# Putting all engines' programs into the entry block without a closing barrier, and issuing the first transfers ahead of the entry barrier

## The chip, the cores and the metric

The kernel runs on one core of one Trainium2 chip. The metric is device time in microseconds (us). The profile's "span" goes from the first to the last instruction of the program; the measured time is longer than it by a rest (1.77 us in the profiled execution of before).

## The reference, cut to what matters

One decode step. A sliding window of attention over a cache (window W = 2048 of 8192 positions, batch 8, 16 key/value heads, 32 query heads, head size 128) and a small MLP (576 to 4608 to 576), mixed by a gate:

```python
q = (x @ wq).reshape(B, 1, 32, 128).transpose(0, 2, 1, 3)
k = repeat(k_cache[:, :, Sk - W:, :], 2, axis=1)      # 67 MB in the window
v = repeat(v_cache[:, :, Sk - W:, :], 2, axis=1)      # 67 MB in the window
p = softmax(einsum("bhqd,bhkd->bhqk", q, k) * Dh ** -0.5)
a = einsum("bhqk,bhkd->bhqd", p, v) ... @ wo
b = gelu(layernorm(x) @ w1 + b1) @ w2 + b2
return g * a + (1 - g) * b                            # g = sigmoid(sum(x * gate_w))
```

With one query per sequence, every byte of the window has to be brought in once. The kernel brings 154.3 MB into the core's memory; its busiest engine, PE, works 69% of the span beside that.

## The kernel before

A planner puts every operation on one engine's list, with its waits; `P.emit` then writes an engine's list out. The parts that the change touches are how the program is opened and how the lists become blocks:

```python
    with ExitStack() as es:
        block = es.enter_context(nc.Block())
        ...
        P.schedule()
        @block.sync
        def _(e):
            P.emit("sp", e, eng_sems, dma_sems)

        @block.gpsimd
        def _(e):
            P.emit("pool", e, eng_sems, dma_sems)
        ... # the same for vector, tensor and scalar
```

What the profile of before shows of this: ahead of the lists, under line 842, four memsets of constants on POOL (96 to 99 ns each), a drain on each of the five engines (7 to 169 ns) and the semaphore instructions of a barrier (17 to 51 ns), the last of them at 0.7 us; behind the lists, under line 223, a branch of the sync engine (42 ns), another drain on each engine (13 to 461 ns) and the semaphore instructions of one more barrier (17 to 51 ns, at 367.4 to 367.5 us). Below, the first group is called the entry block and the entry barrier, the second the end block and the closing barrier.

The first transfers on the lists, and the last operation:

```python
d_x = dma("act", lambda e: e.dma_start(x_sb, x2), "x", ...)
d_gw, d_gw1 = ...            # gate_w, on the Scalar engine's queue
d_b1 = dma("act", ...)
d_wqr = dma("sp", lambda e: e.dma_start(wq_r, A_wq[512:576, :]...), "wq", ...)   # 512 KB
d_wqm = dma("sp", lambda e: e.dma_start(wq_m..., A_wq[0:512, :]...), "wq", ...)  # 4 MB
d_w1m, d_w1r = ...           # 4.5 MB and 576 KB of w1, on the same queue
...                          # then K, V, wo, b2, w2, all on the sync engine's queue
fin.append(dma(eng, ... out2[:, JN * j:JN * j + JN] ...))   # one output DMA each from sync and Scalar engine
add("sp", lambda e: None, deps=fin, name="final_wait", cost=0.05)
```

The last line makes the sync engine wait until both output transfers have landed.

## Time and profile before

| | before |
|---|---|
| measured time, median of 6 runs (lowest to highest) | 369.18 us (369.00 to 369.29) |
| profiled execution: measured time, span | 369.27 us, 367.5 us |
| bytes moved, rate over the span | 154.59 MB, 421 GB/s |
| time that the sync engine's packets took, as a share of the 16 DMA engines' span | 98.6% |
| first packet of wq | 1.82 us after the start of the span |
| last packets of the output | 366.68 us |

These are lines of the page of the kernel before. The second gives busy time, share of the span and number of instructions for each engine; the fourth gives, for the sync engine's queue, packets, megabytes and the share of the 16 DMA engines' time; the fifth splits the chain of work that ended last by what it waited for.

```profile
span 367.5 us, 4111 instructions
PE 254.8 (69%) x1815; PEld 87.3 (24%) x1429; DVE 210.1 (57%) x253; ACT 47.8 (13%) x117; POOL 37.6 (10%) x163
...
DMA packets 11851, 154.59 MB, mean 421 GB/s; under 512 B 1292, under 2 KB 1332, under 8 KB 3000
...
q1 hardware_dynamic: 11776, 154.29, 98.6%
...
DMA 74%; DVE 12%; PE 11%; SPq 1%; ACT 1%; issue 1%; DVEq 0%; ACTq 0%
```

The engines have time to spare (PE, the busiest, works 69%) and the queue has almost none (98.6%). From 20 to 350 us the stream brought in 429 GB/s, at a DMA share of 1.01; that a higher rate could not be had is not shown by any run. At this rate the time is: what passes before the first byte, plus 154.3 MB at the stream's rate, plus what passes after the last byte.

The two ends, then. This is the timeline of the kernel before at its start (start us, duration us, engine, line, operation; SPq and ACTq are the sequencers of the sync and the Scalar engine, and a DMA line there is the issue, not the transfer):

```profile
0.31 0.10 POOL L842 MEMSET const-float32-0.0<- 128x1 f32 x1 [0.31 <-issue]
...
0.79 0.39 SPq L401 DMA_DIRECT2D arena<-in_A_wq_dram  x1
0.79 0.59 ACTq L395 DMA_DIRECT2D arena<-in_A_x_dram  x1
1.24 0.42 SPq L402 DMA_DIRECT2D arena<-in_A_wq_dram  x1
...
1.70 0.42 SPq L404 DMA_DIRECT2D arena<-in_B_w_dram  x1
...
9.24 0.29 DVE L411 COPY arena<-arena 8x64 bf16<-8x64 bf16 x2 [9.24 <-DMA arena<-in_gate_w_dram]
```

And these are the instructions of the entry block, asked for by their source line (duration ns as min/median/max, then first and last start in us):

```profile
L842 SPq DRAIN  x1: 7/7/7, 0.0 to 0.0; - x1
...
L842 ACTq DRAIN  x1: 8/8/8, 0.1 to 0.1; - x1
...
L842 POOLq DRAIN  x1: 169/169/169, 0.4 to 0.4; - x1
...
L842 SPq EVENT_SEMAPHORE  x1: 17/17/17, 0.7 to 0.7; - x1
```

The reader should see a sync engine that is ready at 0.0 us, needs 7 ns for its drain, and then waits in the barrier, where POOL with its constants is the last to end its drain (at 0.54 us; the other four end theirs by 0.32). It is let go at 0.7 us, when nothing that it is about to issue needs those constants.

The end, in the same two views; line 223 is the line that opened the block, so its instructions are those of the closing branch and of the end block:

```profile
364.18 0.96 PE L559 MATMUL ps<-arena 128*8 128x288 bf16 x10 [0.66 <-DMA arena<-in_B_w_dram]
...
365.28 0.45 DVE L783 CAST arena<-ps 8x288 bf16<-8x288 f32 x1 [9.86 <-PE ps L559]
365.69 0.31 ACTq L786 DMA_DIRECT2D out_dram<-arena  x1
365.75 0.32 SPq L786 DMA_DIRECT2D out_dram<-arena  x1
```

```profile
L223 ACTq DRAIN  x1: 241/241/241, 366.0 to 366.0; - x1
L223 SPq COMPARE_BRANCH  x1: 42/42/42, 367.1 to 367.1; - x1
L223 SPq DRAIN  x1: 13/13/13, 367.3 to 367.3; - x1
L223 SPq EVENT_SEMAPHORE  x1: 17/17/17, 367.5 to 367.5; - x1
...
L223 PEldq EVENT_SEMAPHORE  x1: 51/51/51, 367.5 to 367.5; - x1
```

The last w2 bytes release PE at 364.18, the outputs are issued at 365.7, and after the first has landed come a branch, a drain and a barrier (from 367.1 to 367.5). The branch is also what waits for the second of the two output transfers (0.2 us in the list of the sync engine's waits).

### The profile page before, as it was taken

The numbers are of one execution on the slowest core, as the hardware profiler recorded it, in microseconds if no ns is written. First come the engines' busy times: TensorE is split into PE (matmuls) and PEld (weight loads), VectorE is DVE, ScalarE is ACT, GpSimd is POOL, SyncE is SP. The second block draws the span as 40 slices with busy tenths as digits, with TensorE's granted clock in tenths as the row PEclk, the third lists the DMA queues.
The fourth block names the chain that finished last, engine by engine and source line by source line (L and its number), as shares of the span: only waits on it lengthen the run. The fifth ranks groups of instructions, "written<-read, shape, count | busy, mean of one in ns | idle before, by whom it ended". The sixth has DMA issues, their size and how long they took to land.

```text
span 367.5 us, 4111 instructions
## 1 busy us (share of the span) xinstructions
PE 254.8 (69%) x1815; PEld 87.3 (24%) x1429; DVE 210.1 (57%) x253; ACT 47.8 (13%) x117; POOL 37.6 (10%) x163
## 2 busy tenths in 40 slices
PE   0349982895598398673986397765966396865995
PEld 0339200131123032010321032111311031214552
DVE  0704699797667754459654764478544864473000
ACT  1010002100300310003000300003100300003200
POOL 7020010011012001000101001010101000000000
PEclk9999998799689879887898879696988789795559
DMA  8999999999999999999999999999999999999994
GB/s 345 428 408 428 428 427 433 432 426 432 435 430 432 422 427 430 432 439 431 426 430 428 422 438 427 430 426 428 433 430 430 428 431 426 433 428 432 418 424 191
DMA packets 11851, 154.59 MB, mean 421 GB/s; under 512 B 1292, under 2 KB 1332, under 8 KB 3000
## 3 DMA queue, kind: packets, MB, share of 16 engines
q1 hardware_dynamic: 11776, 154.29, 98.6%
q8 instruction: 13, 0.21, 0.2%
q10 hardware_dynamic: 56, 0.03, 0.1%
q14 instruction: 6, 0.05, 0.0%
HBM read 154.31 MB, written 0.01 MB: 420 GB/s over the span
## 4 chain that ended last, share of the span: by engine, by line
DMA 74%; DVE 12%; PE 11%; SPq 1%; ACT 1%; issue 1%; DVEq 0%; ACTq 0%
DMA arena<-in_A_k_cache_dram 50%; DMA arena<-in_B_w_dram 15%; DMA arena<-in_A_v_cache_dram 9%; DVE arena L660 9%; PE ps L173 5%; PE ps L516 2%; PE ps L677 1%; DVE arena L605 1%; PE ps L700 1%; SPq L765 1%; ACT arena L619 1%; DVE arena L624 1%; PE ps L518 1%; PE ps L715 1%; DVE arena L614 0%
## 5 line engine op out<-in xcount | busy, mean ns | idle before, releaser
L660 DVE STREAM_TRANSPOSE arena<-arena 128x2048 f32<-128x2048 f32 x64 | 145.2, 2297 | 78.9 <-DMA arena<-in_A_k_cache_dram 71.5
L173 PE MATMUL ps<-arena 128*128 128x512 bf16 x401 | 134.4, 445 | 15.3 <-DVE arena L660 9.8
L677 PE MATMUL ps<-arena 128*128 128x512 bf16 x115 | 51.8, 450 | 16.7 <-DVE arena L660 16.6
L709 ACT ACTIVATE arena<-ps 128x512 f32<-128x512 f32 x32 | 19.1, 598 | 196.7 <-PE ps L700 196.7
L677 PEld LDWEIGHTS ps<-arena 128*128 128x128 bf16 x128 | 14.6, 114 | 125.8 <-issue 66.8
L715 PE MATMUL ps<-arena 128*128 128x8 f32 x256 | 36.9, 275 | 8.7 <-ACT arena L709 7.7
L653 POOL COPY arena<-arena 32x32 bf16<-32x32 bf16 x128 | 26.0, 203 | 159.2 <-PE ps L173 144.6
L715 PEld LDWEIGHTS ps<-arena 128*128 128x128 f32 x256 | 35.6, 217 | 22.4 <-ACT arena L709 16.4
L700 PE MATMUL ps<-arena 128*32 128x512 bf16 x512 | 36.7, 413 | 6.0 <-DMA arena<-in_A_v_cache_dram 6.0
L669 PE MATMUL ps<-arena 128*128 128x512 bf16 x6 | 3.5, 585 | 37.8 <-DVE arena L624 37.8
L605 DVE TENSOR_REDUCE arena<-ps 128x1 f32<-128x2048 f32 x8 | 18.3, 2282 | 15.5 <-PE ps L173 15.5
L619 ACT ACTIVATE arena<-ps,arena 128x512 bf16<-128x512 f32 x32 | 21.6, 686 | 41.4 <-DVE arena L614 41.4
L700 PEld LDWEIGHTS ps<-arena 128*32 128x32 bf16 x512 | 11.3, 100 | 39.8 <-issue 24.1
L624 DVE STREAM_TRANSPOSE arena<-arena 128x512 bf16<-128x512 bf16 x32 | 19.8, 674 | 0.9 <-ACT arena L619 0.9
L733 POOL TENSOR_TENSOR arena<-arena 128x16 bf16<-128x16 f32 x15 | 4.0, 267 | 142.3 <-ACT arena L725 142.3
L516 PE MATMUL ps<-arena 128*128 128x8 bf16 x144 | 10.9, 201 | 4.5 <-DMA arena<-in_B_w_dram 4.5
L559 PE MATMUL ps<-arena 128*8 128x288 bf16 (+1 forms) x140 | 11.6, 315 | 1.9 <-DMA arena<-in_B_w_dram 1.7
L516 PEld LDWEIGHTS ps<-arena 128*128 128x128 bf16 x144 | 10.8, 159 | 5.0 <-DMA arena<-in_B_w_dram 5.0
L669 PEld LDWEIGHTS ps<-arena 128*128 128x128 bf16 x8 | 0.9, 107 | 45.1 <-DVE arena L624 45.1
L733 DVE TENSOR_TENSOR arena<-ps,arena 128x16 bf16<-128x16 f32 x1 | 0.2, 229 | 19.4 <-PE ps L715 19.4
L438 PE MATMUL ps<-arena 8*128 8x8 bf16 x8 | 0.5, 168 | 13.5 <-DVE arena L411 9.8
L631 DVE RECIPROCAL arena<-ps 128x32 f32<-128x32 f32 x8 | 2.9, 358 | 10.5 <-PE ps L629 10.5
(83 smaller groups left out, 95.6 us busy)
## 6 DMA issues: line engine op xcount, KB each, us to landing
arena<-in_A_k_cache_dram SPq DMA_DIRECT2D x32, 2048.0 KB, 35.8
arena<-in_A_v_cache_dram SPq DMA_DIRECT2D x32, 2048.0 KB, 36.7
arena<-in_B_w_dram SPq DMA_DIRECT2D x1, 4608.0 KB, 24.3
arena<-in_A_wq_dram SPq DMA_DIRECT2D x1, 4096.0 KB, 13.1
arena<-in_B_w_dram SPq DMA_DIRECT2D x3, 1296.0 KB, 33.9
arena<-in_B_w_dram SPq DMA_DIRECT2D x2, 576.0 KB, 28.7
arena<-in_A_wq_dram SPq DMA_DIRECT2D x1, 512.0 KB, 3.7
arena<-in_B_w_dram SPq DMA_DIRECT2D x1, 432.0 KB, 30.4
```

The costliest lines, as they stand in the source:

```text
L173: return e.add_instruction(mybir.InstMatmult(name=nc.get_next_instruction_name(), engine=mybir.EngineType.PE, ins=[e.lower_ap(rhs), e.lowe ...
L516: ins = e.matmul(out_, lhsT, yT[:, kt, :], start=(kt == 0), stop=False)
L559: ins = e.matmul(ps[32 * j:32 * j + 8, BK_ACC, 0:JN], lhsT, rhs[:, JN * j:JN * j + JN], start=False, stop=True, skip_group_check=True, til ...
L605: mx = add("dve", lambda e: e.tensor_reduce(out=k(MX), in_=ps[:, 0:4, :].rearrange("p a n -> p (a n)"), axis=AXL.X, op=ALU.max), deps=[qk_ ...
L619: return e.activation(out=Pm[:, 512 * c:512 * c + 512], in_=ps[:, c, :], func=ACTF.Exp, bias=k(NB), scale=SCALE, accum_out=k(SUM + c))
L624: pts.append(add("dve", (lambda c=c: lambda e: e.transpose(bass.AP(arena, offset=aoffs("PT") + 2048 * (g % 2) + 128 * c, ap=[[AST, 128], [ ...
L653: return e.tensor_copy(dst, src)
L660: tr = add("dve", (lambda h=h, kb=kb: lambda e: e.transpose(bass.AP(arena_f, offset=foffs("KT") + kb * 2048, ap=[[AST // 2, 128], [1, 2048]]),
L677: mm = e.matmul(*args, start=False, stop=last) if rc == 0 else held_matmul(nc, e, *args, stop=last)
L700: mm = e.matmul(ps[c:c + 32, BK_OS[i % 2], :], PT[:, g % 2, 512 * q + 32 * t:512 * q + 32 * t + 32], slot(s)[:, 512 * t:512 * t + 512], st ...
L709: u_ev[i] = add("act", lambda e: e.activation(out=EV[:, i % 2, :], in_=ps[:, BK_OS[i % 2], :], func=ACTF.Copy), deps=[prev] + ([u_sum[i - ...
L715: mm = e.matmul(ps[:, BK_S, OC + 16 * (item % 2) + 8 * (q % 2):OC + 16 * (item % 2) + 8 * (q % 2) + 8], EV[:, i % 2, 128 * r:128 * r + 128 ...
```

## The change

Its intent is to take fixed costs off both ends of the stream. There are no blocks any more: all lists are emitted into the entry block, so the branches, the drains of the end block and the closing barrier go (the profile of after has no instruction of line 223). And the first three transfers (two of wq, one of x) are moved in front of their engine's drain, so ahead of the entry barrier. They need nothing that the barrier guards.

```diff
     with ExitStack() as es:
-        block = es.enter_context(nc.Block())
-
         R = {}
 ...
         P.schedule()
-        @block.sync
-        def _(e):
-            P.emit("sp", e, eng_sems, dma_sems)
 ...         (the same for the other four engines)
+        entry = nc.cur_bb.bb.instructions
+        n_entry = len(entry)
+        handles = {"sp": nc.sync, "act": nc.scalar, "pool": nc.gpsimd, "dve": nc.vector, "pe": nc.tensor}
+        for eng in ENGS:
+            P.emit(eng, handles[eng], eng_sems, dma_sems)
+        for etype, count in ((mybir.EngineType.SP, 2), (mybir.EngineType.Activation, 1)):
+            first = [i for i in entry[n_entry:] if i.engine == etype][:count]
+            assert all(isinstance(i, mybir.InstDMACopy) for i in first)
+            for i in first:
+                entry.remove(i)
+            at = next(n for n, i in enumerate(entry) if i.engine == etype and isinstance(i, mybir.InstDrain))
+            entry[at:at] = first
```

The order of work on each engine is otherwise the same.

More of the change, by code (lines that the diff above doesn't have):

```diff
@@ L789, in build_kernel @@
         P.schedule()
-        @block.sync
-        def _(e):
-            P.emit("sp", e, eng_sems, dma_sems)
-        @block.gpsimd
-        def _(e):
-            P.emit("pool", e, eng_sems, dma_sems)
-        @block.vector
-        def _(e):
-            P.emit("dve", e, eng_sems, dma_sems)
-        @block.tensor
-        def _(e):
-            P.emit("pe", e, eng_sems, dma_sems)
-        @block.scalar
-        def _(e):
-            P.emit("act", e, eng_sems, dma_sems)
+        entry = nc.cur_bb.bb.instructions
[10 more added lines that the diff above has]
+            entry[at:at] = first
     return P
```

## The prediction

> **What bounds the kernel now.** The DMA stream. The page gives 154.59 MB at a mean of 421 GB/s over a span of 367.5 us; the sync engine's queue is busy for 98.6% of it. In 10 us windows from 2 to 352 us the DMA share is 0.94 to 1.05 in every one, so the queue never runs dry. [...] PE is busy 69%, DVE 57%; the chain of waits is 74% DMA. Only what lies before the first byte, after the last byte, or changes the rate can change the time.
>
> **The two ends** (timeline, and the entry block's instructions). The sync engine's drain is at 0.0 us, POOL's constant memsets and drain end at about 0.6, the barrier is released at 0.7; the first wq transfer is issued at 0.79 (392 ns on the sequencer), the second at 1.24 (418 ns), w1 at 1.70. The first DMA packets show between 1.7 and 1.8 us, 0.9 us after the first issue. At the end the last w2 data releases PE at 364.18, the output DMAs are issued at 365.69 and 365.75, their wait ends at about 367.1, then come a branch (367.1), a drain (367.3) and the closing barrier (367.4 to 367.5).
>
> **What the change does.**
> 1. Both wq transfers are issued from about 0.0 instead of 0.79 us: about 0.75 us gained at the head of a saturated stream. The barrier moves later: the sync engine spends 0.39 + 0.06 + 0.42 = 0.87 us on its issues before it arrives, so release at 0.9 to 1.05 instead of 0.7, and w1 is issued at about 1.05 instead of 1.70. wq's 4.7 MB are 11 us of stream, so w1 still queues in time.
> 2. POOL's arena memsets start 0.2 to 0.3 us later; x lands earlier, gate_w about as before. Neither matters: the q projection (17.1 us on) and h projection (to 38.6 us) free buffers long before the queue needs them.
> 3. The closing branch, drain and barrier go: 0.35 to 0.4 us after the output wait. [...] The measured 369.21 us is 1.7 us above the span; I assume that this rest stays.
>
> **On the critical path:** nearly all of it, 0.75 at the head (everything later is paced by the stream) and 0.35 at the tail; the 361 us of stream between stay. That is 1.1 to 1.2 us, 0.3%.
>
> **Predicted time:** 368.05 us, 8 in 10 between 367.5 and 368.8. Faster by over 2%: 0.01; within 2%: 0.98; slower by over 2%: 0.01.
>
> **What would show each step.** Head: first wq issue at 0.0 to 0.1 us, first packets at about 0.9. Barrier: released near 1.0. Middle: the same GB/s, the last w2 release 0.7 to 0.8 us earlier (about 363.4). Tail: no drain or barrier after the output wait; span about 366.35 us.
>
> **What would make it wrong.** The measured time may start or end elsewhere than the span, hiding the head start or the missing barrier (then 0.4 or 0.75 us alone). [...] The small loads' new place in the queue, or the thinning out of the stream from 361 to 364 us, may shift by some tenths. A DMA issued as the very first instruction may be slower than 392 ns.

What the forecast's sum came to: the span of 367.5 us, less 1.1 to 1.2 us (0.75 at the head, 0.35 to 0.4 at the tail), is about 366.35 us, and with the rest of 1.7 us on top 368.05 us. The 369.21 us are the median of the three runs of before that were known then. With them went the reason given for the closing barrier being redundant: that it could go was the author's assumption.

## The result, and the profile after

| | before | after |
|---|---|---|
| measured time, median of 6 runs | 369.18 us | 367.71 us |
| lowest to highest | 369.00 to 369.29 | 367.48 to 368.24 |
| profiled execution: measured time | 369.27 us | 367.59 us |
| profiled execution: span | 367.5 us | 366.3 us |
| rest of that execution (measured time minus span) | 1.77 us | 1.29 us |

The ratio of after to before is 0.9962, with a 95% interval of 0.995 to 0.9975; it agrees with the ratio of the means of the six runs (367.77 over 369.16), so it is not quite the ratio of the medians. The change is 0.4% faster: real, and inside the 2% that counts as "same".

The page of the kernel after, the same lines:

```profile
span 366.3 us, 4121 instructions
PE 259.2 (71%) x1837; PEld 87.4 (24%) x1429; DVE 210.1 (57%) x253; ACT 47.8 (13%) x117; POOL 37.5 (10%) x163
...
DMA packets 11851, 154.59 MB, mean 422 GB/s; under 512 B 1292, under 2 KB 1332, under 8 KB 3000
...
q1 hardware_dynamic: 11776, 154.29, 98.9%
...
DMA 74%; DVE 12%; PE 12%; SPq 1%; issue 1%; DVEq 0%
```

Same packets, same bytes, the same limit. (The 22 more PE instructions are not added work: PE's list of operations is the same, so these records are missing from the trace of before.)

Its timeline at the start:

```profile
0.00 0.39 SPq L399 DMA_DIRECT2D arena<-in_A_wq_dram  x1
0.12 0.58 ACTq L393 DMA_DIRECT2D arena<-in_A_x_dram  x1
...
0.45 0.42 SPq L400 DMA_DIRECT2D arena<-in_A_wq_dram  x1
1.27 0.57 ACTq L394 DMA_DIRECT2D arena<-in_gate_w_dram  x2
...
1.27 0.33 SPq L402 DMA_DIRECT2D arena<-in_B_w_dram  x1
...
10.10 0.29 DVE L409 COPY arena<-arena 8x64 bf16<-8x64 bf16 x2 [10.10 <-DMA arena<-in_gate_w_dram]
```

The instructions of the entry barrier, which are now those of line 833:

```profile
L833 POOLq DRAIN  x1: 169/169/169, 0.4 to 0.4; - x1
...
L833 ACTq DRAIN  x1: 138/138/138, 0.7 to 0.7; - x1
L833 SPq DRAIN  x1: 125/125/125, 0.9 to 0.9; - x1
L833 SPq EVENT_SEMAPHORE  x1: 17/17/17, 1.2 to 1.2; - x1
```

And the end, with the waits on semaphores of the sync engine below it (line 153 is the helper that emits all waits; 366.1 is the start of the last one, the wait for both output transfers):

```profile
363.37 0.96 PE L557 MATMUL ps<-arena 128*8 128x288 bf16 x10 [0.61 <-DMA arena<-in_B_w_dram]
...
364.47 0.44 DVE L781 CAST arena<-ps 8x288 bf16<-8x288 f32 x1 [9.70 <-PE ps L557]
364.89 0.31 ACTq L784 DMA_DIRECT2D out_dram<-arena  x1
364.94 0.32 SPq L784 DMA_DIRECT2D out_dram<-arena  x1
```

```profile
L153 SPq EVENT_SEMAPHORE  x39: 17/17/202, 40.7 to 366.1; - x39
```

The first issue moved from 0.79 to 0.00, the last w2 release from 364.18 to 363.37. After the output wait there is nothing left: no branch, no drain, no barrier. The 202 ns are that wait's own record, the last of the program: it starts at 366.14, when the first of the two output transfers has landed, and ends 0.02 us after the second one's last semaphore update, at 366.32.

**Does the head start survive 360 us of stream?** The trace keeps a record of every packet. The sync engine's queue has 11776 packets and 154.29 MB in both traces; sorted by their ends and summed up, they tell when how much had arrived (interpolated between packets; the output's packets are in it, at the very end):

| arrived, MB | before, us | after, us | earlier by, us |
|---|---|---|---|
| first packet starts | 1.82 | 1.02 | 0.80 |
| 0.5 | 3.77 | 3.09 | 0.68 |
| 4.7 (about all of wq) | 13.96 | 13.21 | 0.75 |
| 15 | 37.98 | 37.29 | 0.69 |
| 40 | 96.21 | 95.45 | 0.76 |
| 80 | 189.52 | 188.66 | 0.85 |
| 120 | 282.56 | 281.92 | 0.64 |
| 154.28 | 364.14 | 363.34 | 0.80 |

The lead is 0.64 to 0.85 us at every point of this table, neither eaten up nor grown; packet by packet it wanders between 0.47 and 0.93 us, with a mean of 0.76. That fits a queue that never runs dry (in the trace of before, the DMA share was 0.94 or more in every 10 us window from 2 to 352 us), which leaves no long pause in which a lead could be lost.

**Where the profiled pair's 1.68 us came from.** From the two traces, with the spans to the hundredth (367.54 and 366.35 us; the page rounds them, so the rest comes out 0.04 us smaller here than in the table above):

| piece | before | after | gain |
|---|---|---|---|
| first output transfer landed (start of the sync engine's last wait record) | 366.94 | 366.14 | 0.80 |
| from there to the end of the span | 0.60 | 0.20 | 0.40 |
| rest: measured time minus span | 1.73 | 1.25 | 0.48 |
| sum | 369.27 | 367.59 | 1.68 |

The first row is the head start. The second is the missing branch, drain and barrier: in both kernels its first 0.20 us are the wait for the second output transfer (to 367.14 and 366.35), and only what follows went away, 0.40 us. The third lies outside the span, where the trace has no instruction to show.

**Where the third part lies.** The packed trace also keeps the times at which semaphores were updated (no view prints them; they can be read from the file). The program names semaphores 96 to 122. Semaphore 2 is not among them, yet it is updated nine times in a row just before the program, nine times around or after its end, and nine times once more at the very end. In us from the first instruction:

| | before | after |
|---|---|---|
| nine updates of semaphore 2 ahead of the program | -0.37 to 0.00 | -0.38 to 0.00 |
| last instruction of the program ends | 367.54 | 366.35 |
| next nine updates of semaphore 2 | 367.87 to 368.31 | 364.51 to 366.63, four of them by 365.63 |
| from the program's end to the ninth | 0.77 | 0.29 |
| from the ninth to the last update of all, another nine of semaphore 2 | 1.15 | 1.15 |
| the last update's time, less the measured time | 0.19 | 0.19 |

So the whole 0.48 us lies between the program's end and the ninth update. The nine updates ahead of the program lie at the same distance from its first instruction in both, the time after the ninth is the same, and the last update lies equally far from the measured time, so nothing is left for the start. In the kernel after, four of the nine updates came (364.51 to 365.63 us) before the sync engine was through with the output (its last wait ends at 366.35), so they are taken here not to be the sync engine's; in the kernel before, none came until 0.33 us after the closing barrier.

**The scatter.** The six runs of the changed kernel differ by 0.76 us, those of before by 0.29. Their spans, and what is left of the measured time:

| run of after | 1 | 2 | 3 | 4 | 5 | 6 |
|---|---|---|---|---|---|---|
| measured, us | 367.59 | 368.24 | 367.48 | 367.84 | 367.87 | 367.57 |
| span, us | 366.3 | 367.0 | 366.2 | 366.5 | 366.6 | 366.3 |
| rest, us | 1.29 | 1.24 | 1.28 | 1.34 | 1.27 | 1.27 |

The rest is steady within 0.1 us, so all of the scatter is inside the span. And the profiled run is one of the fast ones: its 1.68 us is a little more than the difference of the medians, 1.47 us.

### The profile page after: what moved, and what is told of

Read it like the earlier page. It is cut to its first block, busy times and chain, and to the rows that moved or that the text cites. A ratio compares the mean times of both kernels' runs of the same rounds, so it can differ in the third digit from the quotient of the medians.

```text
span 366.3 us, 4121 instructions
## 1 busy us (share of the span) xinstructions
PE 259.2 (71%) x1837; PEld 87.4 (24%) x1429; DVE 210.1 (57%) x253; ACT 47.8 (13%) x117; POOL 37.5 (10%) x163
## 3 DMA queue, kind: packets, MB, share of 16 engines
q1 hardware_dynamic: 11776, 154.29, 98.9%
## 4 chain that ended last, share of the span: by engine, by line
DMA 74%; DVE 12%; PE 12%; SPq 1%; issue 1%; DVEq 0%
DMA arena<-in_A_k_cache_dram 50%; DMA arena<-in_B_w_dram 15%; DVE arena L658 9%; DMA arena<-in_A_v_cache_dram 9%; PE ps L173 5%; PE ps L514 2%; PE ps L675 2%; DVE arena L603 1%; PE ps L698 1%; DVE arena L622 1%; SPq L763 1%; PE ps L516 1%; PE ps L713 1%; DVE arena L612 0%; PE ps L667 0%
## 5 line engine op out<-in xcount | busy, mean ns | idle before, releaser
L173 PE MATMUL ps<-arena 128*128 128x512 bf16 x408 | 136.1, 448 | 0.0
L675 PE MATMUL ps<-arena 128*128 128x512 bf16 x128 | 57.4, 449 | 24.3 <-DVE arena L658 24.2
L667 PE MATMUL ps<-arena 128*128 128x512 bf16 x8 | 4.7, 585 | 41.2 <-DVE arena L622 41.2
```

Source lines behind the costliest of these rows:

```text
L173: return e.add_instruction(mybir.InstMatmult(name=nc.get_next_instruction_name(), engine=mybir.EngineType.PE, ins=[e.lower_ap(rhs), e.lowe ...
L675: mm = e.matmul(*args, start=False, stop=last) if rc == 0 else held_matmul(nc, e, *args, stop=last)
```

## The experiments

None of them ran. Five kernels were written and submitted 24 times over more than four hours, under labels from e1 to o1; no chip took any of them. Four are shown here; the fifth was a second control, the changed kernel with the edit below. The expectations say what would tell the explanations apart. None of them is evidence.

What they were to settle is the 0.48 us outside the span. Theory A puts it at the end: without a closing barrier, four engines finish early (in the trace of after their last instructions end at 346.3, 364.3, 364.9 and 365.2 us, the sync engine's at 366.3; in that of before all five end within 0.1 us, in the closing barrier) and are through with whatever follows the program before the sync engine ends. The trace of before shows that something does follow it: nine updates of semaphore 2 within 0.44 us (367.87 to 368.31), and an update of nearly every semaphore from 7 to 255 within 0.66 us (368.21 to 368.87). Theory B puts it at the start, where issuing from the first instruction might hide something that lies before the span. Theory C credits the missing branches and blocks.

One edit was needed in all of them: the four wo loads of the original use a hand-set shape of the destination that could not be built anew, so they were rewritten as a plain access pattern for the same bytes. What that costs no run shows; the 0.5% in the expectations is the author's guess.

```diff
-            src = bass.AP(A_wo.tensor, offset=128 * h0 * D, ap=[[4 * D, 32], [128 * D, WO_CH], [1, 4 * D]])
-            d = dma("sp", lambda e: run_dma(nc, e, dst[:, :, 0:D], src, (AST, ...)),
+            src = bass.AP(A_wo.tensor, offset=128 * h0 * D, ap=[[D, 128], [128 * D, WO_CH], [1, D]])
+            d = dma("sp", lambda e: e.dma_start(dst[:, :, 0:D], src),
```

The control, the kernel before with that edit alone:

> Control. The kernel before, with only the four wo loads written as a plain access pattern (same bytes, same destination, rows of 1152 bytes at the source instead of 4608), because the loads of the original can't be built anew. Both theories: within 0.5% of before, since the stream stays full: 369 to 371 us. All other runs carry the same wo loads and are to be compared with this one. Span 1.7 to 1.8 us below the measured time, as in before.

Not run. Then the open end without the early issue: the changed kernel without its loop that moves instructions.

```diff
-        for etype, count in ((mybir.EngineType.SP, 2), (mybir.EngineType.Activation, 1)):
-            first = ...      (the whole loop of the change)
```

> The entry block without the closing barrier, but nothing issued ahead of the entry barrier. Theory A (the rest of 0.45 to 0.5 us that the change gained outside the span comes from its end: without the closing barrier the other engines are through with whatever follows the program before the sync engine is): span 0.35 to 0.4 us shorter than j1 and measured time minus span 1.25 to 1.35 us, so 0.8 to 0.9 us below j1. Theory B (the rest comes from the start: issuing from the first instruction hides something before the span): only 0.35 to 0.4 us below j1, measured time minus span stays near 1.75 us. First packets at about 1.7 us in both.

Not run. The early issue without the open end: blocks, branches and closing barrier as before, the three transfers moved from their bodies into the entry block.

```diff
+    for eng, etype, count in (("sp", mybir.EngineType.SP, 2), ("act", mybir.EngineType.Activation, 1)):
+        first = [i for i in bodies[eng] if i.engine == etype][:count]
 ...         (a check of what was found; above, each body's list is kept in `bodies`)
+        for i in first:
+            bodies[eng].remove(i)
+        at = next(n for n, i in enumerate(entry) if i.engine == etype and isinstance(i, mybir.InstDrain))
+        entry[at:at] = first
```

> The three transfers issued ahead of the entry barrier, but blocks, branches and closing barrier kept. Theory A: span 0.7 to 0.8 us shorter than j1, measured time minus span near 1.75 us, so 0.7 to 0.8 us below j1. Theory B: the same span, measured time minus span near 1.3 us, so 1.2 to 1.3 us below j1. First packets at about 1.0 us, barrier released at about 1.2 us in both. If the wider scatter of the changed kernel comes from the early issue, it shows here and not in j3.

Not run. The changed kernel with the barrier alone put back, which was meant to split theory A from both others in one run:

```diff
         for eng in ENGS:
             P.emit(eng, handles[eng], eng_sems, dma_sems)
+        nc.all_engine_barrier()
```

> The changed kernel with one barrier of all engines added again at the end of the entry block; no blocks, no branches, the three early transfers stay. The four wo loads are written as a plain access pattern (same bytes and destination), which should cost under 0.5% and not touch either end. Theory A (the 0.45 to 0.5 us that the change gained outside the span come from the missing closing barrier: the other engines are through with whatever follows the program before the sync engine is): measured time minus span goes back to 1.7 to 1.8 us, and the span ends 0.3 to 0.4 us after the output wait. Theory B (they come from the start, where issuing from the first instruction hides something that lies before the span), and theory C (they come from the missing branches and blocks): measured time minus span stays at 1.25 to 1.35 us, the span ends 0.3 to 0.4 us after the output wait as well. Scatter: if the open end makes the wider scatter of the changed kernel (0.76 us over six runs, against 0.29 before), the five runs here scatter by under 0.3 us; if the early issue makes it, by over 0.5 us. In all: first packets at about 1.0 us.

Not run either. So the split of the 1.68 us is read from the two traces. The semaphore updates rule out theory B for the profiled pair: the nine updates ahead of the first instruction are unchanged, and the 0.48 us lie behind the last. They show the overlap of theory A for the nine updates, not for what follows them. How much of the 0.48 us the missing barrier brings and how much the missing branches (theory C) is not separated by any run.

## Why the prediction was right or wrong

The forecast was 368.05 us, between 367.5 and 368.8, within 2%. Measured were 367.71 us. The median lies in the range (one run of the six, 367.48 us, just below it); one term of the sum was wrong, by some 0.4 us, against a forecast gain of 1.1 to 1.2.

1. **The bound: right.** It said that only the two ends or the rate can change the time. The rate is the same (421 and 422 GB/s over the span), and the lead of the stream stays between 0.64 and 0.85 us at all the points of the table.
2. **The head: right, 0.75 us forecast, 0.80 us measured** (issue 0.79 to 0.00, first wq packet 1.82 to 1.02, output wait 366.94 to 366.14). The forecast time of the first packet, 0.9 us, was 0.1 us too early. The packets that it had read at 1.7 to 1.8 us in the trace of before were those of x, on the Scalar engine's queue (1.74); wq's first came at 1.82. The worry that a DMA as the very first instruction might be slow was idle: its issue took 391 ns, against 392 before. From the end of the issue to the first wq packet it was 0.63 us, and 0.65 before; from its start 1.02 and 1.04.
3. **The barrier: right in kind, short in size.** Forecast was a release at 0.9 to 1.05 us and the w1 issue at 1.05; measured were 1.2 and 1.27. The step that failed took the drains as they stood in the entry block before, 7 and 8 ns. Behind a DMA issue the sync engine's drain took 125 ns and started at 0.9, and the Scalar engine's took 138. The trace of before had a hint of this at its other end, where the Scalar engine's drain behind its output DMA took 241 ns. It cost nothing here, as forecast: w1 joined a queue that still held almost all of wq, of which 0.5 MB had arrived by 3.09 us.
4. **"x lands earlier, gate_w about as before": right for x, wrong for gate_w, and harmless.** x was issued 0.67 us earlier (0.12 against 0.79), yet its first packet started at 2.03 us, against 1.74 before, and the first eight packets of 1152 bytes on that queue, which by their order and size are x's eight rows, had arrived by 2.52, against 2.87. gate_w released the Vector engine at 10.10 instead of 9.24. The program waits for x and gate_w together, so moving x gained nothing. From the end of its issue to x's first packet it was 1.34 us, and 0.36 before. In the trace of before, x's packets start 0.08 us ahead of wq's; in that of after, 1.01 us behind them. Why they came so late no run here shows. What it did downstream can be followed: the projection of q began at 17.98 us instead of 17.13, and the sync engine's wait for it grew, as the list of its waits shows (total us, times, longest us), of before and of after:

```profile
SPq L645 <- PE ps L484: 17.0, 1, 17.0
```

```profile
SPq L643 <- PE ps L482: 18.1, 1, 18.1
```

   This wait ends near 22 us. By then 16.3 MB had been put into the queue (wq, w1 and three K loads), and the last of them arrives at about 40 us, an estimate from the table above (15 MB at 37.29, 40 MB at 95.45, so 2.3 us for each further MB). There were some 18 us of slack, and 0.85 us of it were used.
5. **The tail inside the span: right,** 0.35 to 0.4 us forecast, 0.40 measured. The forecast span was 366.35; the profiled one is 366.3, the median of the six is 366.4.
6. **"I assume that this rest stays": wrong.** The measured time was taken as span plus 1.7 us. The rest was 1.77 us in the one execution of before that was profiled, and 1.24 to 1.34 us in all six runs of after. This term, 0.4 to 0.5 us, is why the median lies 0.34 us below the forecast. The prediction named the risk only in one direction: that something outside the span could hide a gain. It did not think of a gain there. What the trace shows in its place: the stretch from the program's end to the ninth update of semaphore 2 shrank from 0.77 to 0.29 us, with four of the nine updates done before the program's end. This is the overlap of theory A, and it leaves no room for theory B; the share of theory C stays open. That the forecast stayed in its range in spite of this owes to the range's width of 1.3 us, not to this step.
7. **The scatter was not forecast.** It lies within the span, over 0.8 us. Which part of the change brings it is open.

## What to carry to other kernels

In this kernel the sync engine's packets took 98.6% of the DMA engines' span and the rate stayed as it was (421 and 422 GB/s over the span); all of the profiled pair's 1.68 us lay in front of the first byte (0.80) and behind the last (0.40 inside the span, 0.48 after it). Where another kernel's profile shows the same, read those two stretches to the hundredth of a microsecond, and try moving the first large transfer in front of anything that it doesn't need. Here a lead of 0.80 us at the head of the stream came out at its end as 0.80, as the arrival table shows, while an issue that was moved 0.67 us earlier on another queue (x) won nothing: gate_w, which is waited for with it, came 0.86 us later. And when a change touches a program's end, don't take the difference between measured time and span as a constant: here it moved by 0.48 us, more than the barrier's own 0.40 us inside the span.
